# A longer warm-up at the head of TensorE's list: 30 products instead of 12

## Chip, cores and metric

The kernel runs on one core of one Trainium2 chip. The metric is device time in microseconds (us) of one execution, as the median of the runs of a kernel; before the change it is 639.57 us over three runs (639.39 to 639.85). A profile is one execution recorded by the hardware profiler. Engines are called as in the profile: PE (TensorE, matmuls), PEld (TensorE's weight loads), DVE (VectorE), ACT (ScalarE), POOL (GpSimd), SP (SyncE, which issues most transfers); a small q behind an engine's name is its sequencer.

## What is computed

A retention block (a decayed recurrent attention) feeds a gated feed-forward block; all is in fp32.

```python
gamma = 1.0 - 2.0 ** (-5.0 - np.arange(H, dtype=np.float32))
for t in range(S):                       # B, H, S, D = 4, 8, 768, 64
    state = gamma[None, :, None, None] * state + np.einsum('bhd,bhe->bhde', k[:, :, t], v[:, :, t])
    y[:, :, t] = scale * np.einsum('bhd,bhde->bhe', q[:, :, t], state)
...
x = np.ascontiguousarray(attn_out.transpose(0, 2, 1, 3)).reshape(B * S, H * D)   # 3072 x 512
g = x @ w_gate                           # 512 x 1536
silu = g * (1.0 / (1.0 + np.exp(-g)))
val = x @ w_val
return (silu * val @ w_out).astype(np.float32)   # w_out 1536 x 512
```

## The kernel before

The 3072 rows are done in four segments of 768 rows (two sequences, three chunks of 128 rows of each). A segment has three kinds of work for TensorE.

- Retention: scores, decayed states and outputs of each chunk, from products of 64 or 128 columns. In segment 0 they stand on lines 651, 713, 728 and 742; in segments 1 to 3 on line 825, a helper `mm` that the functions `scores_of`, `low`, `old` and `grow` call for products of 64 x 64 with 64 columns. One call of a mixing function issues 32 to 160 of them in a row.
- Up: `w_gate` and `w_val` times x for twelve blocks of 128 hidden columns, each fp32 operand split into parts so that TensorE can work on 32-bit reduced values: three matmuls per product. Segment 0 does this plainly (lines 1057 and 1075, 384 and 256 columns); segments 1 to 3 with seven block products instead of eight (line 1230, 384 columns).
- Down: the hidden values times `w_out` (line 1301, 512 columns), with the parts of the down weights read back from DRAM into the ring `oitem` (line 1278, source `wdnt`).

The order in which the functions run, and so the order of each engine's list, is written out by hand in the string `PLAN`; retention of segment s+1 is woven into the down stage of segment s. So in the stretches from 127 to 186 us, 285 to 338 us and 440 to 493 us TensorE's list alternates between runs of 64-column products (line 825) and groups of 512-column products (line 1301), which take very different times per instruction. SP's list is in the same order: loads for the next segment (lines 816 and 820) stand between loads of down weights (line 1278).

TensorE's list begins with a warm-up. `warm_up(n, cols)` on line 1417 issues n products of the tile `warm` with itself into bank 3; `warm` is cleared by DVE on line 1435, and nothing reads what the products write: bank 3 is written anew afterwards. They depend on nothing else, and fill the time in which the first inputs are on their way. Each product in fp32 is two weight loads and two matmuls in the trace (lines L1420: 24 and 24 for 12 products). After them the first scores (line 651) wait for `in_k_t` and `in_q_t`.

## Time and profile before

| | before |
|---|---|
| median of 3 runs | 639.57 us (639.39 to 639.85) |
| span of the profiled execution | 641.7 us |
| PE busy | 630.8 us, 5601 matmuls |
| PEld busy | 581.7 us, 5601 weight loads |
| DVE, ACT, POOL busy | 506.9, 396.6, 173.2 us |
| instruction queue q8 | 44 packets, 0.72 MB |
| instruction queue q14 | 23 packets, 0.19 MB |

Of the profiled execution only its span is listed (from the first to the last recorded instruction); it is 2.1 us longer than the median of the runs, which were executed without the profiler, so the two are not compared with each other directly. Rows of the timeline give start and length in us, engine, line, operation, tiles, shape, count, and in brackets how long the engine was idle before and what ended that wait ("issue": nothing that the profile shows). Rows of the chain of waits give start, length and what the end of the program depended on. Rows of windows give the stretch, its length, then busy time and number of instructions of PE, PEld, DVE, ACT and POOL, the granted clock of TensorE (1.00 is full), the share of the DMA engines that was busy, and GB/s. Rows of DMA queues give packets, MB, and their share of sixteen DMA engines' time; rows of DMA issues give tiles, queue, count, KB and the median time from issue to landing.

### The profile page before, as it was taken

What the parts mean: (1) busy time and instruction counts of PE and PEld (TensorE: products, weight loads), DVE (VectorE), ACT (ScalarE), POOL (GpSimd) and SP (SyncE); (2) the same over time, 40 slices, a digit from 0 to 9 for tenths busy, and PEclk for the clock granted to TensorE, in tenths of its full rate; (3) what the DMA queues carried; (4) which work ended last, traced back from release to release, by engine and by line L of the source; (5) the groups of instructions that cost most, each with busy time, mean ns of one, the idle gap of its engine ahead of it and who ended that gap; (6) DMA issues with size and microseconds to landing.
All of it is one profiled execution on the core that took longest, in us unless ns stands there. A gap on an engine that the chain in (4) does not pass through costs nothing.

```text
span 641.7 us, 14131 instructions
## 1 busy us (share of the span) xinstructions
PE 630.8 (98%) x5601; PEld 581.7 (91%) x5601; DVE 506.9 (79%) x764; ACT 396.6 (62%) x845; POOL 173.2 (27%) x117
## 2 busy tenths in 40 slices
PE   7999999999999999999899999999999999999997
PEld 6899999987789999997788999998888999999886
DVE  4998788899898889887489777978778888877551
ACT  4786897677866665667376664756764655564220
POOL 0544455544423531210001343340002014232000
PEclk9999999999999999999899999999999999999999
DMA  9899998689788443688783435577785345304764
GB/s 319 289 353 311 372 333 274 259 323 305 281 278 305 140 157 115 214 263 239 204 312 130 179 115 206 173 203 229 229 290 196 113 149 189 128 13 140 230 212 149
DMA packets 57747, 143.03 MB, mean 223 GB/s; under 512 B 5840, under 2 KB 28368, under 8 KB 57680
## 3 DMA queue, kind: packets, MB, share of 16 engines
q1 hardware_dynamic: 57104, 141.33, 64.5%
q8 instruction: 44, 0.72, 0.5%
q10 hardware_dynamic: 576, 0.79, 0.3%
q14 instruction: 23, 0.19, 0.1%
HBM read 112.21 MB, written 29.88 MB: 221 GB/s over the span
## 4 chain that ended last, share of the span: by engine, by line
PE 94%; DMA 5%; ACT 1%; SPq 1%; issue 0%; DVE 0%; ACTq 0%
PE bank L1230 41%; PE bank L1301 30%; PE bank L1057 13%; PE bank L825 5%; PE bank L1075 3%; DMA oitem<-wdnt 2%; DMA hT<-in_v_n_dram 2%; PE bank L742 1%; DMA hT<-in_q_t_dram 1%; PE bank L728 0%; SPq L820 0%; PE bank L713 0%; PE bank L651 0%; ACT gitem L1129 0%; ACT local L871 0%
## 5 line engine op out<-in xcount | busy, mean ns | idle before, releaser
L1301 PE MATMUL bank<-oitem,gitem 128*128 128x512 f32 (+1 forms) x873 | 205.9, 393 | 3.0 <-DMA oitem<-wdnt 2.9
L1301 PEld LDWEIGHTS bank<-oitem,gitem 128*128 128x128 f32 x873 | 161.9, 189 | 38.1 <-DMA oitem<-wdnt 3.5
L1230 PE MATMUL bank<-xa,gitem 128*128 128x384 f32 x864 | 160.6, 334 | 0.0
L1230 PEld LDWEIGHTS bank<-xa,gitem 128*128 128x128 f32 x864 | 150.6, 188 | 0.1
L1135 POOL TENSOR_TENSOR gitem<-gitem 128x768 fp32r<-128x768 f32 x36 | 72.1, 2007 | 185.0 <-DVE gitem L1132 165.7
L1135 POOL TENSOR_TENSOR oitem<-oitem 128x512 fp32r<-128x512 f32 (+1 forms) x48 | 52.8, 1105 | 168.1 <-DVE oitem L1132 148.0
L418 DVE SCALAR_TENSOR_TENSOR gitem<-gitem 128x768 fp32r<-128x768 f32 x84 | 86.6, 1041 | 1.7 <-DVE gitem L1132 0.5
L1057 PE MATMUL bank<-xa,oitem 128*128 128x384 f32 x480 | 84.2, 335 | 0.0
L1230 PE MATMUL bank<-xb,gitem 128*128 128x384 f32 x432 | 83.7, 335 | 0.0
L1057 PEld LDWEIGHTS bank<-xa,oitem 128*128 128x128 f32 x480 | 83.0, 188 | 0.2
L1230 PEld LDWEIGHTS bank<-xb,gitem 128*128 128x128 f32 x432 | 75.8, 188 | 0.4
L1129 ACT ACTIVATE gitem<-loads 128x768 fp32r<-128x768 f32 x72 | 59.1, 842 | 25.7 <-PE bank L1230 16.9
L1132 DVE SCALAR_TENSOR_TENSOR gitem<-gitem,loads 128x768 fp32r<-128x768 f32 x72 | 70.5, 991 | 3.4 <-ACT gitem L1129 3.3
L1132 DVE SCALAR_TENSOR_TENSOR gitem<-gitem,hT 128x768 fp32r<-128x768 f32 x48 | 46.2, 965 | 28.0 <-ACT gitem L1129 24.1
L1129 ACT ACTIVATE gitem<-hT 128x768 fp32r<-128x768 f32 x48 | 40.2, 844 | 43.7 <-PE bank L1301 35.3
L1230 PE MATMUL bank<-xb,oitem 128*128 128x384 f32 x216 | 43.0, 335 | 0.0
L1230 PEld LDWEIGHTS bank<-xb,oitem 128*128 128x128 f32 x216 | 38.0, 188 | 0.0
L1246 ACT COPY tmp<-bank 128x384 f32<-128x384 f32 x36 | 17.3, 480 | 27.0 <-PE bank L1230 22.9
L1247 DVE TENSOR_TENSOR hT<-bank,tmp 128x384 f32<-128x384 f32 x36 | 20.0, 554 | 16.5 <-PE bank L1230 16.4
L1245 ACT COPY tmp<-bank 128x384 f32<-128x384 f32 x36 | 17.2, 479 | 24.8 <-PE bank L1230 17.1
L1249 DVE TENSOR_TENSOR hT<-hT,bank 128x384 f32<-128x384 f32 x36 | 19.7, 550 | 13.4 <-ACT bank L1249 13.2
L1247 ACT COPY tmp<-bank 128x384 f32<-128x384 f32 x36 | 17.3, 481 | 16.5 <-PE bank L1230 11.9
(152 smaller groups left out, 807.2 us busy)
## 6 DMA issues: line engine op xcount, KB each, us to landing
loads<-wup SPq DMA_DIRECT2D x36, 896.0 KB, 5.4
oitem<-wdnt SPq DMA_DIRECT2D x33, 768.0 KB, 4.7
wdnt<-oitem SPq DMA_DIRECT2D x12, 768.0 KB, 5.8
wup<-first SPq DMA_DIRECT2D x9, 896.0 KB, 6.9
rawp<-in_w_gate_dram SPq DMA_DIRECT2D x12, 512.0 KB, 7.3
rawp<-in_w_val_dram SPq DMA_DIRECT2D x12, 512.0 KB, 6.6
rawp<-in_w_out_dram SPq DMA_DIRECT2D x12, 512.0 KB, 5.8
out_dram<-chunk_x SPq DMA_DIRECT2D x21, 256.0 KB, 4.7
```

What stands on the lines that cost most here:

```text
L418: stt(o, x, 1.0, y, op0=mul, op1=op)
L825: nc.tensor.matmul(o, a, b, start=start, stop=True, skip_group_check=True)
L1057: nc.tensor.matmul(o, w[:, a, ts(b, P)], X0[:, a, i, NC - 1 - b], start=a == b == 0, stop=a == 2 and b == NC - 1, skip_group_check=True)
L1075: nc.tensor.matmul(o, w[:, a, ts(b, P)], X0[:, a, :, NC - 1 - b, ts(j, P)], start=a == b == 0, stop=a == 2 and b == NC - 1, skip_group_che ...
L1129: act(o[0], x, AF.Copy, scale=CUT / FAR)
L1132: stt(o[1], f32(o[0]), -FAR, x, op0=mul, op1=add)
L1135: op(o[2], f32(o[0]), f32(o[1]), op=add)
L1230: nc.tensor.matmul(o, w[:, a, k], x[:, a, KH - 1 - k], start=start and a == k == 0, stop=a == 2 and k == KH - 1, skip_group_check=True)
L1246: lambda: act(gate, c11, AF.Silu, scale=ONE), lambda: copy(u2, x),
L1247: lambda: copy(p5, wb), lambda: tt(h1, x, p5, op=add),
L1249: lambda: act(x, x, AF.Silu, scale=ONE), lambda: tt(h1, h1, x, op=mul))
L1301: nc.tensor.matmul(o, hs[g][:, a, ds(i * TH + u * P, P)], wo[g][:, a, cols], start=n == 0 and (f == 0 or final), stop=f == NF - 1 and a == ...
```

## The change

The warm-up issues 8 products of 128 columns and 22 of 16 columns, where it was 7 and 5. Nothing else is touched: the other engines' lists, TensorE's products behind the warm-up and their order are the same. TensorE's list becomes longer by 18 products, 72 instructions by the count above, and each instruction behind the warm-up stands 72 places later in it.

```diff
     nc.vector.memset(warm, 0.0)
     nc.scalar.activation(warm[:, ds(P, 1)], warm[:, :1], AF.Silu)
-    warm_up(7)
-    warm_up(5, 16)
+    warm_up(8)
+    warm_up(22, 16)
     for f in range(NF):
         up(f, T0 + UP0 * (f - NPF))
```

## The prediction

> **What bounds the kernel now.** I read the page first, then the chain of waits, then stretches of the timeline, and last the DMA queues in narrow windows.

> ```profile
> span 641.7 us, 14131 instructions
> PE 630.8 (98%) x5601; PEld 581.7 (91%) x5601; DVE 506.9 (79%) x764; ACT 396.6 (62%) x845; POOL 173.2 (27%) x117
> PEclk9999999999999999999899999999999999999999
> q8 instruction: 44, 0.72, 0.5%
> ```

> TensorE (PE) is busy for 98% of the span at the full clock; only one slice of forty shows less than 9. Whatever is won or lost must therefore be time in which TensorE stands still, and there are 641.7 - 630.8 = 10.9 us of it. The fourth row is the one the change is about: TensorE's 5601 weight loads and 5601 matmuls, 11202 instructions, come with 44 packets on the instruction queue, 0.72 MB / 44 = 16.4 KB each. 11202 / 44 = 255, so a packet is a block of 256 instructions of 64 bytes (semaphore instructions, which the rows do not count, make up the rest). A packet costs 0.5% x 16 engines x 641.7 us / 44 = 1.17 us of one DMA engine.

> The chain of waits shows where TensorE stands still:

> ```profile
> 10.63 7.57 DMA hT<-in_v_n_dram
> 18.24 1.09 PE bank L742 x16
> ...
> 299.44 7.44 DMA oitem<-wdnt
> 306.92 14.84 PE bank L1301 x57
> ...
> 448.31 2.02 PE bank L825 x126
> 450.33 0.20 issue
> 450.53 0.74 PE bank L825 x31
> ```

> Up to 18.24 us the inputs' loads set the pace. From there TensorE leads, but for a load of down weights (`oitem<-wdnt`) that lands at 306.88, and for a small hole at 450.33 that no engine and no transfer explains.

> **The hole at 450.33 is a late block of instructions.** The timeline of TensorE there, first its matmuls, then its weight loads:

> ```profile
> 442.53 5.78 PE L1301 MATMUL bank<-oitem,gitem 128*128 128x512 f32 x24
> 448.24 1.16 PE L825 MATMUL bank<-loads 64*64 64x64 f32 x64
> 449.22 0.65 PE L825 MATMUL bank<-tab,loads 64*64 64x64 f32 x32
> ...
> 450.04 0.29 PE L825 MATMUL bank<-loads,local 64*64 64x64 f32 x6
> 450.53 0.21 PE L825 MATMUL bank<-loads,local 64*64 64x64 f32 x1 [0.20 <-issue]
> ```

> ```profile
> 450.53 0.13 PEld L825 LDWEIGHTS bank<-loads,local 64*64 64x64 f32 x1 [0.35 <-issue]
> ```

> It lies inside a run of eight equal products, between the sixth and the seventh, where nothing is waited for. 64 of these matmuls start within 449.22 - 448.24 = 0.98 us, 15 ns apart; the seventh was due at 450.04 + 6 x 0.015 = 450.13 and came at 450.53: **0.40 us lost**. 256 instructions of such small products are 128 pairs, about 2 us; of the large products of line 1301 (24 in 5.7 us) they are 30 us. So a block is used up fastest where small products stand in a row, and only there can the next one be late. The DMA queues in two windows, 443.8 to 447.7 and 447.7 to 449.2, have:

> ```profile
> q1 hardware_dynamic: 400, 0.95, 74.2%
> ...
> q1 hardware_dynamic: 354, 0.40, 94.1%
> q8 instruction: 1, 0.02, 4.3%
> ```

> One block came in the second window, none in the first; the seventh product followed about 1.3 us after that window's end. My reading, which no row shows outright: two blocks are held, and on entering a block the list asks for the one after it. Then the time that a block lasts is the time that the next fetch has. I place the borders by the hole (one at 450.5, the others 256 places from each other) and cut windows there; x is the number of instructions:

> ```profile
> 135.70:140.40 4.70, 4.70 (x146) 3.85 (x136) 4.57 (x8) 3.17 (x9) 1.42 (x1) 1.00 0.76 294
> 176.10:181.80 5.70, 5.70 (x147) 4.60 (x140) 5.70 (x9) 2.25 (x4) 1.30 (x1) 1.00 0.99 361
> 447.70:450.40 2.70, 2.63 (x129) 2.13 (x128) 1.76 (x3) 2.65 (x10) 0.00 (x0) 1.00 0.89 230
> ```

> These hold the shortest block, 2.7 us, the one that ends in the hole, and two of the next; no other hole lies on a border.

> **The change, part by part.** *The list.* In the trace a warm-up product is two weight loads and two matmuls (below: 24 of each for 12 products). 18 more products are 72 instructions, so every border falls 72 places, 36 pairs, earlier in the work. The border at 450.5 moves to 449.6, and the one at 447.7 moves back over 12 small pairs and all 24 large ones of line 1301 to 442.2. The run of small products is thus split between two blocks, each with 24 large products in it. Windows cut at the new borders, the two shortest blocks and the one before the hole:

> ```profile
> 133.00:138.80 5.80, 5.80 (x132) 4.25 (x134) 5.67 (x10) 4.98 (x16) 1.37 (x2) 1.00 0.97 374
> 293.10:299.40 6.30, 6.20 (x143) 5.33 (x136) 3.79 (x7) 4.73 (x15) 0.00 (x0) 1.00 0.86 213
> 442.20:449.60 7.40, 7.40 (x144) 6.06 (x140) 6.79 (x11) 4.78 (x15) 0.00 (x0) 1.00 0.67 202
> ```

> The shortest block now lasts 5.8 us instead of 2.7. Blocks of 4.7 and 5.7 us show no hole before, so I expect none at 5.8 and more: **-0.40 us**, and since TensorE leads from there to the end, nothing takes it back. Bounds: 0 if the hole only moves, and more than 0.40 if other executions fetch more slowly than the profiled one.

> [...]

> *The products themselves.* TensorE's first rows:

> ```profile
> 1.08 3.06 PEld L1420 LDWEIGHTS bank<-warm 128*128 128x128 f32 x14 [1.08 <-DVE warm L1435]
> 1.08 3.70 PE L1420 MATMUL bank<-warm 128*128 128x128 f32 x24 [1.08 <-DVE warm L1435]
> 4.37 0.31 PEld L1420 LDWEIGHTS bank<-warm 128*16 128x16 f32 x10 [0.23 <-issue]
> 5.93 1.16 PE L651 MATMUL bank<-hT 64*128 64x128 f32 x16 [1.14 <-DMA hT<-in_k_t_dram]
> ```

> The eighth wide product is two more pairs of 3.06 / 14 = 0.22 us; the narrow ones take at most 0.31 / 10 = 0.031 us a pair. The warm-up then ends at 4.78 + 0.44 + 34 x 0.031 = 6.27 us by this upper price, 0.34 us after the first score product is due (5.93, waiting for its load); with the narrow pairs at 0.024 us, the start-to-start that ten in 0.31 us leave when the last one's own length is taken off, it ends near 6.0. I take 0: even 0.34 us lies ahead of 18.24, where TensorE waits for `in_v_n` issued at 10.63, which does not depend on TensorE. With that cover gone it would cost up to 0.34 us.

> *Sum*: 641.7 - 0.4 = 641.3 in the profiled execution. Its span is 2.1 us above the median of the runs; no separate time of it is listed, so I carry the difference over: 639.57 - 0.40 = **639.2 us**.

> **The rivals.** *One: the moved fetch runs into the tight weight loads (slower).* The load that lands at 306.88 is needed around 303.9. The next block was fetched right behind it; the queues in the windows 299 to 306.9 and 306.9 to 307.1:

> ```profile
> q1 hardware_dynamic: 1037, 2.23, 94.8%
> ...
> q8 instruction: 1, 0.02, 37.9%
> ```

> 36 pairs earlier that block's border falls at 299.4 instead of 301.8 (windows above and below), just ahead of the load issued at 299.44, and the fetch may be served first. A packet holds one DMA engine for 1.17 us; if it pushes back that engine's part of the load, the load lands 1.17 us later, and so again one of the weight loads that follow it, since the next border moves back towards this stretch as well, by 36 large pairs (24 in 5.7 us), some 8.6 us. 639.2 + 1.2 = 640.4, or 641.5 with both. Against it: a fetch of 1.17 us costs nothing where the engine that carries it has slack. It decides if the load's landing moves by more than 1 us.

> *Two: the wait at 306.88 gets shorter (faster).* Loads of this form take 4.7 us in the median, this one 7.44:

> ```profile
> oitem<-wdnt SPq DMA_DIRECT2D x33, 768.0 KB, 4.7
> ...
> 306.92 5.12 PEld L1301 LDWEIGHTS bank<-oitem,gitem 128*128 128x128 f32 x16 [3.30 <-DMA oitem<-wdnt]
> ...
> 308.00:312.00 4.00, 4.00 (x12) 3.17 (x11) 3.08 (x4) 1.32 (x5) 0.00 (x0) 0.57 0.64 180
> ```

> After the wait the granted clock falls: over the 4 us of the last row it is 0.57 in the mean, so 4 x 0.43 = 1.7 us of full clock are missing. If the pending fetch is what held up the load's engine, asking for it earlier frees it: -2.7 us of wait and -1.7 of slow clock, 639.2 - 4.4 = 634.8; the wait alone, 636.5. Against it: the runs' 639.57 may already lack this wait, being 2.1 us below the span.

> *Three: a slow fetch meets a block of 6 to 7 us.* The block before the one that was fetched at 306.9, in a window cut at its borders:

> ```profile
> 293.70:301.80 8.10, 8.00 (x139) 6.51 (x134) 6.19 (x10) 6.67 (x20) 0.00 (x0) 1.00 0.83 202
> ```

> So the fetch was asked for at about 301.8 and came at 306.9: 5.1 us, with 1.2 for the packet and 1.3 until use 7.6. Against the 6.3 us of the block from 293.1 that is a hole of 1.3 us: 640.5. Before, the block from 301.8 held the long wait and lasted far longer, so it cost nothing.

> *Four: the list's place does not matter*, and the hole at 450.33 has a cause that no row shows and that stays where it is: 639.6. Against it speaks that the hole has no releaser.

> **How the numbers follow.** Forecast 0.48, rival two 0.20, rival one 0.17, rival three 0.10, rival four 0.05. 0.2%, about what a measurement can tell from no change, is 1.3 us. Faster by more: rival two and 0.08 of the forecast, where other executions lose more at the borders, 0.28. Slower by more: the two-load form of rival one and the upper ends of one and three, 0.20. Within: 0.52. The range goes from the wait alone of rival two, 636.4, to both loads of rival one, 641.5; it leaves out the lower half of rival two and the tails.

> **What would show it.** Right: no "issue" hole near 450, 44 fetches as before, 60 warm-up matmuls, and the row at 5.93 with almost no idle time before it. Wrong in the first step: a hole of the same kind on a border 256 places from another. Rival one: the loads after 299 land later relative to their issue. Rival two: full clock in the slice around 305. The forecast is wrong if the wait at 306.9 differs by more than a microsecond.

## The result and the profile after

| | before | after |
|---|---|---|
| median, both kernels on one chip, 21 runs each | 639.26 us (637.84 to 641.18) | 640.39 us (639.21 to 643.81) |
| ratio of the times, 95% interval | | 1.0023 (1.0012 to 1.0033) |
| span of the profiled execution | 641.7 us | 642.0 us |

The changed kernel is slower by 0.23%, some 1.4 us, where 0.4 us less was forecast (the ratio is of the means; the medians differ by 1.1 us). In two later batches its ratio to before was 1.0016 (0.9999 to 1.0032) and 1.0027 (1.0014 to 1.0039).

The page of the changed kernel, in the rows that were shown of before:

```profile
span 642.0 us, 14203 instructions
PE 632.1 (98%) x5637; PEld 583.1 (91%) x5637; DVE 504.8 (79%) x764; ACT 396.4 (62%) x845; POOL 172.4 (27%) x117
PEclk9999999999999999999999999999999999999999
q8 instruction: 44, 0.72, 0.5%
```

14203 - 14131 = 72 instructions more, half matmuls and half weight loads, and still 44 fetches. Now the chain of waits of the changed kernel, where it differs:

```profile
6.93 6.15 DMA hT<-in_k_t_dram
13.08 0.14 issue
13.21 1.16 PE bank L651 x16
...
183.15 1.38 issue
184.53 0.97 PE bank L825 x49
...
449.16 2.49 PE bank L825 x160
```

The hole at 450 is gone: 160 small products now run in one piece of 2.49 us, where before 2.02 + 0.20 + 0.74 = 2.96 us passed for 157 of them. But two stops are new. The timeline of TensorE shows them with what they waited for:

```profile
1.09 4.77 PE L1420 MATMUL bank<-warm 128*128 128x128 f32 x60 [1.09 <-DVE warm L1435]
6.01 1.16 PE L651 MATMUL bank<-hT 64*128 64x128 f32 x16 [0.15 <-DMA hT<-in_k_t_dram]
...
10.82 0.69 PE L713 MATMUL bank<-hT 128*64 128x64 f32 x16
13.21 1.16 PE L651 MATMUL bank<-hT 64*128 64x128 f32 x16 [1.70 <-DMA hT<-in_k_t_dram]
...
182.69 0.46 PE L825 MATMUL bank<-loads,states 64*64 64x64 f32 x15
184.53 0.27 PE L825 MATMUL bank<-loads,states 64*64 64x64 f32 x1 [1.38 <-issue]
```

The first is a wait of 1.70 us for a load of k_t, issued at 6.93. The second looks like the old hole: between the fifteenth and the sixteenth of sixteen equal products, with no releaser. Counted in the instructions of the two traces, its place is 19 x 256 ahead of the place that the old hole had, to within one, so I take it for a border, and for a late block again.

The DMA queues, in windows around the first fetch and around the one that the second stop waited for, show when the blocks came; of the changed kernel, 7.1 to 10.36, 10.36 to 11.5, 173 to 182.2 and 182.2 to 183.3 us:

```profile
q1 hardware_dynamic: 949, 1.20, 108.6%
...
q8 instruction: 1, 0.02, 2.1%
q1 hardware_dynamic: 235, 0.43, 100.1%
...
q1 hardware_dynamic: 964, 2.92, 93.7%
...
q1 hardware_dynamic: 108, 0.45, 100.6%
q8 instruction: 1, 0.02, 5.4%
```

and of the kernel before, 4 to 15.9 and 15.9 to 17.1 us:

```profile
q1 hardware_dynamic: 3075, 4.21, 100.6%
q10 hardware_dynamic: 158, 0.27, 6.0%
...
q1 hardware_dynamic: 246, 0.45, 100.1%
q8 instruction: 1, 0.02, 5.9%
```

So the first block is fetched at 10.4 us instead of 15.9, and the queues are full by this view (100% and more) all that time. What one packet does in a full queue is seen in the landing of the loads on the 16 DMA engines, from the trace's records of each load's 16 landings:

```
load, issued at                eighth engine   15th    last
before   k_t    6.85              11.22        11.84   11.86
before   v_n   10.63              16.12        16.75   18.20
after    k_t    6.93              11.40        11.74   13.08
after    v_n   10.54              16.27        16.62   18.02
```

TensorE's waits for two of these loads ended just behind the last landing: at 18.24 us behind 18.20 before, at 13.21 behind 13.08 after. One engine is 1.3 to 1.5 us behind the rest; the landings don't name their engines, and I take it for the one that carried the block. It is behind from the fetch on, and every load queued behind it is late by that much: in the first trace of before the loads issued from 10.63 to 18.22 us, by 1.45 to 1.51, and in that of the changed kernel those issued from 6.93 to 17.37, by 1.34 to 1.44. Before, this began with the v_n load issued at 10.63, and made the wait at 18.24 that the prediction took for given; now it begins with the k_t load issued at 6.93.

How long TensorE took from one product to the next of a fixed list of products, in the traces of this study that the argument needs (worked out from the matmul records, warm-up left out; the column heads give the places that the list is moved by; the last row ends with the start of the last product; "72 n" is a warm-up of narrow products alone, "72 t" has the table piece later):

```
stage, by times of     0      0      0     72     72     72    72 n   72 t    48
the first trace      before again  wide  after  again  third               
0 to 46.3            46.28  45.80  46.09  47.71  46.70  46.49  46.80  46.42  46.12
46.3 to 126.9        80.62  80.62  80.62  80.62  80.62  81.56  81.13  80.62  80.62
126.9 to 181.1       54.22  54.24  54.22  54.48  54.66  54.26  55.08  54.20  54.63
181.1 to 184.1        2.94   2.94   3.03   4.60   2.94   2.94   2.94   2.94   2.94
184.1 to 196.3       12.25  12.25  12.25  12.26  12.25  12.25  12.65  12.59  12.25
196.3 to 230.2       33.86  33.86  33.85  33.86  34.51  33.91  34.39  34.31  33.86
230.2 to 303.7       73.49  73.16  73.17  73.34  73.17  73.17  73.16  73.18  73.19
303.7 to 346.1       42.41  38.93  37.68  40.05  37.67  38.06  38.17  39.09  38.67
346.1 to 447.7      101.63 101.91 101.61 101.63 101.61 101.65 101.65 101.65 101.63
447.7 to 452.0        4.32   4.24   4.04   3.84   3.84   4.55   4.61   3.84   4.42
452.0 to the end    186.16 186.14 186.13 186.12 186.08 186.24 186.11 186.20 186.11
```

Read it by rows. The weight wait at 304 us (row 303.7 to 346.1) differs by 4.7 us between executions of one and the same list: it hides everything else when two single traces are subtracted, and the change has no visible part in it. What goes with the places are the first row and, in three of the five traces with 72 places, the row from 196.3; what came once is the hole in the row from 181.1. The 4.55, 4.61 and 4.42 in the row from 447.7 hold waits for weights of 0.5 to 0.7 us, not the hole.

### The profile page after: what moved, and what is told of

It reads as the page before. It is cut to its first block, busy times and chain, and to the rows that moved or that the text cites. A ratio compares the mean times of both kernels' runs of the same rounds, so it can differ in the third digit from the quotient of the medians.

```text
span 642.0 us, 14203 instructions
## 1 busy us (share of the span) xinstructions
PE 632.1 (98%) x5637; PEld 583.1 (91%) x5637; DVE 504.8 (79%) x764; ACT 396.4 (62%) x845; POOL 172.4 (27%) x117
## 4 chain that ended last, share of the span: by engine, by line
PE 94%; DMA 3%; ACT 1%; SPq 0%; issue 0%; DVE 0%; ACTq 0%
PE bank L1230 41%; PE bank L1301 29%; PE bank L1057 13%; PE bank L825 6%; PE bank L1075 3%; DMA oitem<-wdnt 1%; DMA hT<-in_k_t_dram 1%; PE bank L742 1%; PE bank L651 1%; DMA hT<-in_q_t_dram 1%; PE bank L728 1%; PE bank L713 0%; SPq L820 0%; ACT states L916 0%; ACT gitem L1129 0%
## 5 line engine op out<-in xcount | busy, mean ns | idle before, releaser
L1301 PE MATMUL bank<-oitem,gitem 128*128 128x512 f32 (+1 forms) x873 | 204.7, 392 | 1.9 <-DMA oitem<-wdnt 1.8
L1301 PEld LDWEIGHTS bank<-oitem,gitem 128*128 128x128 f32 x873 | 160.8, 188 | 36.9 <-DMA oitem<-wdnt 2.4
L1230 PEld LDWEIGHTS bank<-xb,oitem 128*128 128x128 f32 x216 | 37.9, 188 | 0.0
L1246 ACT COPY tmp<-bank 128x384 f32<-128x384 f32 x36 | 17.2, 478 | 27.0 <-PE bank L1230 22.9
L1245 ACT COPY tmp<-bank 128x384 f32<-128x384 f32 x36 | 17.2, 478 | 25.0 <-PE bank L1230 17.2
L1247 ACT COPY tmp<-bank 128x384 f32<-128x384 f32 x36 | 17.3, 479 | 16.5 <-PE bank L1230 11.7
## 6 DMA issues: line engine op xcount, KB each, us to landing
oitem<-wdnt SPq DMA_DIRECT2D x33, 768.0 KB, 4.8
wdnt<-oitem SPq DMA_DIRECT2D x12, 768.0 KB, 6.0
```

Source lines behind the costliest of these rows:

```text
L1230: nc.tensor.matmul(o, w[:, a, k], x[:, a, KH - 1 - k], start=start and a == k == 0, stop=a == 2 and k == KH - 1, skip_group_check=True)
L1245: steps = (lambda: copy(p1, x), lambda: tt(c11, z, p1, op=add), lambda: act(gate, c11, AF.Silu, scale=ONE), lambda: copy(u2, x), lambda: c ...
L1247: lambda: copy(p5, wb), lambda: tt(h1, x, p5, op=add),
L1301: nc.tensor.matmul(o, hs[g][:, a, ds(i * TH + u * P, P)], wo[g][:, a, cols], start=n == 0 and (f == 0 or final), stop=f == NF - 1 and a == ...
```

## The experiments

All ratios are against the kernel before, run in turn on the same chip. The theory that the experiments test is this: the change costs by the places of the list, because the blocks of TensorE's list are fetched at other moments and so come to lie ahead of other loads in the DMA queues; the warm-up's own length doesn't matter.

**1. Pad in the first wait.** The warm-up stays; 18 narrow products go where TensorE waited for v_n.

```diff
-    C0:0 o2 U1:1 m2 o3
+    C0:0 o2 w18 U1:1 m2 o3
-        "w": lambda n: warm_up(1),
+        "w": lambda n: warm_up(n, 16),
```

> The warm-up stays 7 products of 128 columns and 5 of 16. Eighteen products of 16 columns (72 places) are put later, where TensorE waits some 1.1 us at 18.24 us, so the first border of the instruction blocks stays where it was before and every later one moves by 72 places. Theory (the 72 places act through the instruction fetches): the first fetch starts at about 16 us as before, the wait for the k_t load at 13 us and its 1.4 us stay away, the hole at 450 us (0.40 us) is gone, and the hole at about 183 us (1.6 us) may come. Median ratio to before 0.9985 to 1.000 without the hole at 183, up to 1.002 with it in most executions. Rival one (the length of the warm-up and the clock's release set the loss, not the list places): ratio 1.000, like before in everything. Rival two (all of the loss is the later borders): ratio 1.002 as the changed kernel.

Ratio 1.002 (1.0004 to 1.0036). By the ratio this is rival two, but the trace shows that the pad wasn't hidden. Its chain of waits begins:

```profile
1.18 4.56 DMA hT<-in_k_t_dram
5.74 0.14 issue
5.88 2.08 PE bank L651 x16
```

The score group took 2.08 us instead of 1.16: TensorE ran slowly at first, came later, asked for the first block later (its packet starts at 16.5 us, behind the v_n load, which landed whole at 16.8), found no wait, and paid for the pad: 18.57 to 19.57 us. The run says nothing on the first stage; it does show no hole at 450 (3.84 us in that row) and 34.30 us in the row from 196.3. It also lost 0.9 us in the row from 184.1, where TensorE waited for ScalarE at 187 us; two other traces with 72 places (experiments 3 and 10) lost 0.3 to 0.4 us at the same place.

**2. A longer warm-up without a move.** Twelve products of 128 columns, the same 48 instructions as before.

```diff
-    warm_up(7)
-    warm_up(5, 16)
+    warm_up(12)
```

> Twelve warm-up products of 128 columns in place of 7 and 5 narrow ones: 48 instructions as before, so no instruction moves, but the warm-up takes longer than before. Theory (instruction fetches): as before, ratio 1.000 within 0.001, first fetch at about 16 us, TensorE's wait for k_t at 13 us not there, the hole at 450 us (0.40 us) there. Rival one (the warm-up's length): ratio 1.002 as the changed kernel.

Ratio 0.9997 (0.9981 to 1.0012), the rows of "wide" in the table as before: the warm-up's length isn't the cause. One thing came out otherwise: no hole at 450. The 0.2 us above 3.84 there are a wait for weights.

**3. The move without the wide products.** Thirty narrow products, 120 instructions, the list moved by 72.

```diff
-    warm_up(7)
-    warm_up(5, 16)
+    warm_up(30, 16)
```

> Thirty warm-up products of 16 columns and none of 128: 120 instructions, every later one moves by 72 places as in the changed kernel, but the warm-up's work is shorter than before. Theory (instruction fetches): as the changed kernel, ratio 1.001 to 1.003, first fetch at about 10 us, a wait of 1.4 to 1.7 us for the k_t load at 13 us, no hole at 450 us. If a shorter warm-up alone mattered (rival one), the loads would not lag, TensorE would start as before and the ratio would follow the granted clock: 1.000, or above 1.005 with a half clock of several us in the first stage.

Ratio 1.0021 (1.0007 to 1.0035): as the changed kernel, with another warm-up. The first fetch starts at 10.1 us and the k_t load's last engine lands at 12.87, 1.25 behind the 15th; but TensorE, slow at the start as in 1 (20 matmuls from 6 to 9 us, where before had 39), only came for it at 13.5.

**4. The changed kernel again.**

> The changed kernel again, beside the other three on the same chip: ratio 1.0012 to 1.0033, first fetch at about 10 us, TensorE's wait of 1.4 to 1.7 us for k_t at 13 us again. Open is whether the hole of 1.6 us at 183 us and the half clock of 3.4 us at 14.5 us come back: if both belong to single executions, this profiled execution is without one of them and its fastest run is still 1 us or more above the fastest of before, from the early wait alone.

Ratio 1.0016 (0.9999 to 1.0032). Its timeline has the wait for k_t again, and neither the hole at 183 nor the half clock:

```profile
10.74 0.69 PE L713 MATMUL bank<-hT 128*64 128x64 f32 x16
13.14 1.16 PE L651 MATMUL bank<-hT 64*128 64x128 f32 x16 [1.71 <-DMA hT<-in_k_t_dram]
```

In the first trace of the changed kernel the granted clock fell after this wait:

```profile
4.00:14.40 10.40, 8.17 (x139) 6.96 (x139) 4.75 (x8) 4.44 (x13) 0.00 (x0) 1.00 1.07 380
14.50:18.00 3.50, 3.50 (x32) 2.97 (x28) 3.50 (x5) 1.87 (x6) 2.08 (x2) 0.51 1.07 376
```

3.5 us at 0.51 are 1.7 us of full clock that are missing; its first stage took 47.71 us, this one's 46.70. The fastest run was 638.94, against 637.40 of before. New is a loss of 0.65 us in the row from 196.3. The chain of waits there:

```profile
191.87 9.62 DMA wdnt<-oitem
...
201.57 0.04 ACT oitem L1129
...
201.89 0.47 ACT tmp L1245
202.36 0.04 issue
202.41 3.76 PE bank L1230 x20
```

A transfer of weights takes 9.62 us, ScalarE's next instruction needs it, and what TensorE waits for stands behind that instruction on ScalarE. In the three traces with the old places (before, experiments 2 and 11) the same transfer took 8.3 to 8.6 us. About half of the difference is the landing of its last engine, 201.49, against 200.71 for the 15th; before it was 199.16 against 198.89. The DMA queues from 191 to 198 us of this kernel:

```profile
q1 hardware_dynamic: 494, 2.82, 97.5%
q8 instruction: 1, 0.02, 0.9%
q14 instruction: 1, 0.01, 0.3%
```

A block of TensorE's list (q8) was fetched there, its packet starting at 196.0 us. Before, that border's packet started at 201.3 to 201.8, behind the transfer, and the DMA queues from 191 to 199.2 us hold none:

```profile
q1 hardware_dynamic: 657, 3.16, 93.0%
q14 instruction: 2, 0.02, 0.5%
```

**5. A move by 256 places**, one whole block, with 76 narrow products.

```diff
-    warm_up(7)
-    warm_up(5, 16)
+    warm_up(76, 16)
```

> Seventy-six warm-up products of 16 columns and none of 128: 304 instructions, so every later instruction moves by 256 places, one whole block, and the borders fall on the same products as before, with one border more inside the warm-up. Theory (what moved is the places of the borders): from 46 us on the stages take as long as before: 57.72 us for the next stage, no wait of 0.4 us or more at 203 us, and the hole at 450 us (0.2 to 0.4 us) is back. In the first stage two fetches now run ahead of early loads, so TensorE reaches the 46 us stage later than before, by 0.5 to 2.5 us; ratio 1.001 to 1.004. Rival (many narrow products, or a longer instruction list, cost something by themselves): the later stages show the waits of the changed kernel and the hole at 450 stays away.

Ratio 1.0013 (0.9992 to 1.0035). The row from 196.3 took 33.83, the first stage 46.66, as the theory has it. The hole at 450 didn't come back (3.84), and the stage from 46.3 to 126.9 took 82.46 instead of 80.62, by two waits for ScalarE at 80 and 97 us behind transfers of weights. The later borders are where they were before, so the places of these borders can't be the cause of that loss; it stays open.

**6. Pad before the fourth score product.** Twelve narrow products where TensorE waits for VectorE (0.36 us idle at 14.53 in the trace of before); bank 2 takes them, as a third argument of the helper, whose own two lines are left out below. Only the later borders move, by 48.

```diff
-    x1:2 s3 x1:1
+    x1:2 w12 s3 x1:1
-        "w": lambda n: warm_up(1),
+        "w": lambda n: warm_up(n, 16, 2),
```

> The warm-up stays as before. Twelve products of 16 columns (48 places, about 0.6 us) are put ahead of the fourth score product, where TensorE waits 0.58 us for VectorE in every trace so far. The first border stays, every later one moves by 48 places; the shortest block by the trace of before would be 6.95 us. Theory (only the first border's place costs, the later borders' places gain): the first stage loses at most 0.1 us, the hole at 450 is gone, ratio 0.9985 to 1.0005. Rival (the later borders' places are what costs, by later waits at 132, 187 and 203 us): ratio 1.001 to 1.002 with those waits in the trace.

Ratio 1.0022 (1.0005 to 1.0039), so the expectation fell. The rival's waits at 132, 187 and 203 us aren't in the trace either (54.36, 12.25 and 33.85 in those rows). The loss stands ahead: 46.87 in the first stage, with TensorE slow until 10 us as in 1 (22 matmuls from 6 to 9 us in both), and 81.80 in the next by waits for ScalarE such as at 96.6 us. One trace can't tell how often either happens with this list. So this list has the ratio of the changed kernel without the wait for k_t and without a fetch ahead of the transfer at 192 us (its packet starts at 199.3).

**7. Twenty places fewer.** Only the seven wide products.

```diff
     warm_up(7)
-    warm_up(5, 16)
```

> Seven warm-up products of 128 columns and no narrow ones: every later instruction moves by 20 places the other way. Theory: the first fetch is asked for some 0.5 us later, after the load of v_n that was issued at 10.63 us, so that load lands whole at about 16.8 us instead of 18.2, TensorE's wait of 1.08 us at 17 us goes or shrinks, and it reaches the stage at 46 us 0.2 to 0.8 us earlier than before. The hole at 450 stays or grows to 0.7 us (the block there shrinks from 6.71 to 4.60 us). Ratio 0.998 to 1.000. Rival (the first fetch's place does not matter): start of the 46 us stage within 0.15 us of before, ratio 1.000 to 1.001.

Ratio 1.0012 (0.9996 to 1.0028). TensorE was slow until 12 us in this trace (22 matmuls from 6 to 9 us), so its first stage (47.37) doesn't tell what the first fetch costs. The landings fit the theory: the first packet starts at 17.2 us, the v_n load lands whole at 16.56, and the late engine begins with the k_t load issued at 11.69 (19.38, against 17.90 for the 15th). The row from 46.3 took 81.36, 0.7 us more than before. The block at 450 is shorter than before, and its hole larger. The timeline:

```profile
447.59 0.30 PE L825 MATMUL bank<-loads,chunk_x 64*64 64x64 f32 x8
448.60 0.58 PE L825 MATMUL bank<-loads,chunk_x 64*64 64x64 f32 x24 [0.71 <-issue]
```

**8. A move by 120 places**, to where a block is shortest.

```diff
-    warm_up(5, 16)
+    warm_up(35, 16)
```

> Seven warm-up products of 128 columns and thirty-five of 16: every later instruction moves by 120 places. By the trace of before a block of only 2.11 us then lies at 292.5 to 294.6 us and one of 4.42 us at 156.4 to 160.8. Theory: its fetch takes some 3 to 5 us from the border to use, so a hole of 1 to 3 us stands at about 295 us in every profiled execution, perhaps one of up to 1 us at 161, and the first stage loses 0.4 us or more; ratio 1.003 to 1.007. If places of borders do not matter: ratio 1.000, no hole there.

Ratio 1.0055 (1.0036 to 1.0075). The hole stands where the count put it. TensorE's timeline, and below it a stretch of windows:

```profile
295.38 0.65 PE L825 MATMUL bank<-loads,chunk_x 64*64 64x64 f32 x28
298.01 0.43 PE L825 MATMUL bank<-loads,chunk_x 64*64 64x64 f32 x4 [1.98 <-issue]
...
298.00:301.50 3.50, 3.49 (x11) 2.73 (x12) 0.77 (x3) 2.19 (x8) 0.00 (x0) 0.51 0.42 119
```

1.98 us without work, and behind them 3.5 us at half clock: this hole cost nearly twice itself. The row from 230.2 took 77.04 instead of 73.2, 3.9 us more, which is all of the ratio. In ten of the twelve runs the mean granted clock was 0.997 or 0.996, as in this trace, which speaks for the hole in most executions. The row from 196.3 took 34.41, with this list's fetch starting at 192.8 us.

**9. A move by 48 places** with a warm-up of the changed kind.

```diff
-    warm_up(7)
-    warm_up(5, 16)
+    warm_up(8)
+    warm_up(16, 16)
```

> Eight warm-up products of 128 columns and sixteen of 16: every later instruction moves by 48 places instead of 72. Theory: the first fetch is asked for at about 8.3 us, after the k_t load that was late in the changed kernel, so TensorE's wait for it at 11 us shrinks from 1.9 to under 0.7 us and the stage at 46 us begins within 0.3 us of before where the clock is full from 5 us on; the border that lay at 194 us in the changed kernel lies after 196, its fetch starts after 198.5 us, behind the weight transfer that ScalarE waits for, so TensorE's wait at 203 us (0.44 to 0.65 us at 72 places) is gone; the hole at 450 is gone. Ratio 0.9985 to 1.0003. Rival (other waits take over: those for ScalarE at 53 to 98 us, 0.9 us with the same later borders): ratio 1.0005 to 1.002.

Ratio 1.0006 (0.9988 to 1.0024), the least of the moved lists. The timeline's wait for k_t is back to its size of before, and at 201 us nothing is waited for:

```profile
12.25 1.16 PE L651 MATMUL bank<-hT 64*128 64x128 f32 x16 [0.49 <-DMA hT<-in_k_t_dram]
...
201.26 4.33 PE L1230 MATMUL bank<-xa,gitem 128*128 128x384 f32 x24
```

The fetch near 196 starts at 198.5 here, the transfer took 8.40 us, and the DMA queues from 191 to 198 us hold no block of q8:

```profile
q1 hardware_dynamic: 522, 2.95, 101.0%
q14 instruction: 1, 0.01, 0.3%
```

Both losses went with 24 places, as the theory has it. The interval leaves open whether this list is as fast as before; it doesn't beat it.

**10. The changed list, with the fifth table piece loaded later**, so that k_t is queued ahead of the first fetch.

```diff
-    A4 A3 l2:1 l2:0 r0
+    A4 l2:1 l2:0 A3 r0
```

> The changed kernel, with the fifth piece of the decay table loaded after q_t and k_t of the third chunk instead of ahead of them; the instruction list and its places are as changed. Theory: k_t is now ahead of the first fetch in its DMA engine's queue and lands at about 11 us on all engines, the table piece takes the late landing (about 13 us, first read at 16 us), TensorE's wait of 1.7 to 1.9 us at 11 us falls below 0.7, and the stage at 46 us begins at 46.0 to 46.4 us where the clock is full, against 46.7 of the changed kernel. The wait at 203 us stays (0.4 to 0.65 us). Ratio 1.000 to 1.002, some 0.4 us below the changed kernel. Rival (the first fetch's late load is not what costs): start of the 46 us stage as changed, ratio 1.001 to 1.0025.

Ratio 1.0024 (1.0007 to 1.0041). k_t landed at 11.33 us on its last engine and the wait for it is gone; the table piece, now behind it, landed 1.03 us behind its 15th engine, at 13.01. But the next load is late as well, and TensorE's timeline has its wait there:

```profile
11.61 1.16 PE L651 MATMUL bank<-hT 64*128 64x128 f32 x16
13.73 1.09 PE L742 MATMUL bank<-tmp,hT 128*64 128x128 f32 x16 [0.97 <-DMA hT<-in_v_n_dram]
```

So the first stage (46.42) gained only 0.28 us on that of experiment 4 and 0.07 on that of experiment 12: all loads queued behind the fetch are late on one engine, and taking one of them out shows the next. 34.31 in the row from 196.3, as expected.

**11. The kernel before again.**

> The kernel of before once more, for its profile. Theory: no wait of 0.3 us or more at 203 us, no wait for k_t above 0.8 us at 11 us but one of about 1 us for v_n at 17 us, the hole at 450 us (0.2 to 0.9 us). Open is whether the waits for ScalarE at 53 to 98 us and for VectorE at 132 us, which some of the other kernels show, come with this list too: if they do, they belong to single executions and not to the places. Ratio 1.000 within 0.002.

Ratio 1.0011 (0.9991 to 1.003). TensorE's timeline in the first stage, for comparison:

```profile
11.75 1.16 PE L651 MATMUL bank<-hT 64*128 64x128 f32 x16 [0.39 <-DMA hT<-in_k_t_dram]
...
17.76 1.09 PE L742 MATMUL bank<-tmp,hT 128*64 128x128 f32 x16 [0.61 <-DMA hT<-in_v_n_dram]
```

No wait at 203, none at 46 to 127 and none at 132; but no hole at 450 either, against the expectation: the 0.40 us above 3.84 there are short waits with a releaser, 0.26 us for a copy by ScalarE and 0.11 for weights. The block in question was asked for as before and came some 3.4 us ahead of its use, where in the first trace it landed at 449.19, and TensorE went on 1.34 us later, at 450.53, after its stop.

**12. The changed kernel a third time.**

> The changed kernel a third time, for its profile and for twelve more times. What belongs to its list should be there again: TensorE's wait of 1.7 us for k_t at 11 us, the start of the 46 us stage at 46.6 to 46.8 us if the clock stays full, ScalarE's wait of 0.7 to 1.0 us for the weight transfer at 201 us and 0.4 to 0.65 us lost behind it, no hole at 450. What belongs to single executions may be missing: the half clock at 14.5 us, the hole at 183 us, the waits for VectorE at 132 us and for weights at 304 us. Ratio 1.001 to 1.003.

Ratio 1.0027 (1.0014 to 1.0039). The wait for k_t is there (1.03 us idle, first stage 46.49), the hole at 450 isn't, nor the half clock, nor the hole at 183. ScalarE's waits from 190 to 206 us:

```profile
ACT xa L1138 <- DVE tmp L418: 1.3, 1, 1.3
...
ACT oitem L1129 <- DMA wdnt<-oitem: 0.4, 1, 0.4
```

The transfer took 9.35 us, but ScalarE lost only 0.4 by it and TensorE 0.05: the lag recurs, its price differs from execution to execution.

## Why the prediction failed, step by step

*What bounds the kernel, and the block of 256 instructions:* held. A list moved by 120 places stopped TensorE for 1.98 us at the border where the count put the shortest block. That two blocks are held was my reading; no row shows it outright. What the first traces of the two kernels show: counted back from each hole, the 256 recorded instructions ahead of it (semaphores included) begin at 447.69 us before and at 173.40 after; a packet starts behind that, at 448.15 and 182.25, and lands at 449.19 and 183.20, and TensorE goes on at 450.53 and 184.53. The 1.98 and 0.71 us idle in experiments 8 and 7 stand at ends of 256 as well.

*"-0.40 us" for the hole at 450:* the mechanism was right, the size wasn't. The hole is gone in all traces with 72 places, but with the borders of before it stands in one of four (before; not in experiments 2, 5 and 11). The term is 0.40 / 4 = 0.1 us on these four, not 0.40. What I took for a cost of the list was a cost of one execution: whether a block is late hangs, by these traces, on how long after its border the packet starts, and I put that down to the DMA queues' load (93.7% from 173 to 182.2 us in the first trace of the changed kernel). At the border ahead of the hole at 183, 8.9 us passed until the packet started in that trace (173.40 to 182.25), at most 1.5 in the second, and some 6 in the third, without a hole. So "the shortest block now lasts 5.8 us" didn't bound the loss: 1.59 us were lost at the end of a block of some 11 us, the hole included. By this reading it is rival three's mechanism at another place, in one of the six traces with these later borders (the three of the changed kernel and experiments 1, 3 and 10).

*"I take 0: even 0.34 us lies ahead of 18.24, where TensorE waits for in_v_n issued at 10.63, which does not depend on TensorE":* this is the step that failed. The time of the products was right (TensorE's first score came at 6.01 instead of 5.93), and so was the cover. But the wait at 18.24 did depend on TensorE's list: it was the mark of the first fetch, which sat just ahead of that load in one DMA engine's queue. Moved 72 places, the fetch sits ahead of the k_t load, and the wait comes at 13 us with 1.0 to 1.7 us. The first stage took 46.70 and 46.49 at full clock against 46.28, 45.80 and 46.09 before: 46.60 - 46.06 = **0.5 us**, and 1.65 where the clock fell behind the wait. Experiments 2 and 3 show that the wait comes with the places and not with the products, 9 and 10 that it is that load and that queue.

*Not in the sum at all:* the fetch that came to lie in front of the weight transfer at 192 us. It cost TensorE 0.44 to 0.65 us in four of the six traces with 72 places (0.05 in experiment 12; none in the first, where TensorE was late by the hole at 183), 0.55 with 120, and nothing with 0, 48, 256 or -20. I had followed the 44 fetches only to where a block is short, and one of them, in rival one, to a transfer that TensorE waits for.

*Rival one* (0.17) had the right mechanism: a fetch holds up one engine's part of a transfer, by 1.0 to 1.5 us here, close to its 1.17. The place was wrong: the weight wait at 304 differs as much within either list as between them. *Rival two's* shorter wait (1.42 us instead of 2.87) and full clock did appear in the trace of the changed kernel, and the forecast's own sign, a wait that differs by more than 1 us, came true; but for the same reason they count for nothing. *Rival four* fell with experiments 3 and 8.

The parts, 0.5 for the first stage, some 0.2 to 0.6 for the transfer, -0.1 for the hole, and 1.6 for one hole in six traces (0.3), make 0.9 to 1.3 us (0.5 + 0.2 - 0.1 + 0.3, and 0.4 more); the runs show some 1.4. The half clock, which isn't among them, adds about 0.2 by an estimate from the run times: in 6 of the 45 runs of the changed kernel the mean granted clock is 0.997, as in its first trace, and without these six the mean falls from 640.96 to 640.75 us; of the 115 runs of before in the experiments' batches one has it (and its first trace, at 308 us).

That the parts come near the total doesn't prove them. Experiment 6 has the same ratio without the two main ones. And the kernel of before may itself lose time that none of its traces shows: of the four traces with its warm-up, two (before and 11) started at full speed and two (experiments 1 and 6) slowly, with 47.60 and 46.87 us in the first stage, their pads included. How often its runs do so is not known. What is shown is the wait for k_t and its cause; the rest of the 1.4 us is in part argued.

Open are also why the clock falls behind the k_t wait in one trace of three, and the waits of 0.4 to 0.9 us at 46 to 127, at 132 and at 187 us, which the changed kernel and other moved lists show in some traces and three traces of unmoved lists in none. Most stand behind transfers of weights, but the list moved by 256 loses the most by them (1.84 us at 46 to 127) with the old borders, so I don't put them down to the borders.

## What to carry to other kernels

A longer instruction list was here a change to the DMA queues: 72 places more moved the first fetch from 15.95 to 10.36 us, ahead of another load. So look where the fetches will start, and which transfers with a waiting reader are queued behind them, above all at the head of the program, where these queues were full (100% and more from 4 to 17.1 us before). A stop in one trace is a sample, as the hole at 450 was, in one of four; before a sum takes it as a gain, see whether a second trace of the same kernel has it. And a wait that seems to be given by the loads alone may be the mark of something that the edit moves, as the one at 18.24 us was: ask why the last of a load's 16 landings is late.
